# First batch of a pooled attention in quarters of half the heads by half the tokens, with keys pooled in turned form

## The chip, the cores and the metric

The kernel runs on one core of one Trainium2 chip. The metric is the device time in microseconds (us) of one execution; of several runs the median is given. Engine names as in the profile: PE is TensorE (matmuls) and PEld its weight loads, DVE is VectorE, ACT is ScalarE, POOL is GpSimd, SP is SyncE. PSUM is the memory that PE writes its results to, in eight banks of 512 fp32 columns; SBUF holds all else.

## What is computed

Eight batches of eight heads, 576 tokens and 64 columns a head go through an attention whose keys and values are first pooled: each row of the pooled keys is the mean of 8 tokens, so 72 rows are left. The result, as 4608 tokens by 512 columns, goes through four experts, each with two products, weighted by normed probabilities.

```python
k_p = k.reshape(B, H, Sp, pool, D).mean(axis=3)          # 72 rows of 8 tokens each
v_p = v.reshape(B, H, Sp, pool, D).mean(axis=3)
scores = scale * np.matmul(q, k_p.transpose(0, 1, 3, 2))
...
attn = np.exp(scores)
attn = attn / (np.sum(attn, axis=-1, keepdims=True) + 1e-09)
return np.matmul(attn, v_p).astype(np.float32)
...
p = domain_probs / (domain_probs.sum(-1, keepdims=True) + 1e-09)
for e in range(E):
    h = np.maximum(x @ w1[e], 0.0)
    out += p[:, e:e + 1] * (h @ w2[e])
```

## The kernel before

The tokens are worked on in nine chunks: the first 512 tokens of each of the eight batches, and a ninth chunk of the 64 left over from each. For a chunk, x is held turned (xT: columns on the partitions, in four blocks KC of 128), so that the up product of an expert gives the hidden values H with the hidden columns on the partitions, and the down product gives rows of the output, which DVE, ACT or POOL add to an accumulator with the probability as a factor. From the second chunk on, the products of an expert go by seven steps with sums of blocks (`up_product`, L680, and `down`, L749). The attention of the next batch is mixed into the products of the present one by slots. All engines work in the order in which the code issues to them; nothing is reordered.

The first batch has no products beside it to be mixed into. `attention_first` (L552) writes its order out by hand, for all engines, from the landing of the queries to the up product of the first expert. It is all that the change rewrites.

- *Loads.* Queries come as fp32 over the queues of SP and ACT (`load_q`, L174) and are rounded to bf16 by DVE and ACT (`round_q`, L188). Keys and values of the first batch (`load_first`, L135), then all weights, come over POOL's queue in the order of lines 1035 to 1048; most of POOL's issues after 15 us wait for an earlier one to land.
- *Queries.* `queries` (L343) turns them on PE, two heads a bank, and DVE and ACT copy them to `qT`.
- *Keys.* The 576 tokens of a head lie as 64 rows of 9 tokens, two heads of a group on partitions 0 to 63 and two on 64 to 127. `sum_pool` (L308) pools them with a matrix of zeros and ones (`takes`) as weights: 9 steps for each of the two halves, 18 matmuls a group of four heads (L314), which give pooled rows on 72 partitions. `sum_keys` (L320) casts them to `kp_all`, each key twice side by side; `keys` (L295) turns four heads with four PE transposes (L304) and one copy (L306) into `kpT`, which then has the key's 64 columns on partitions 0 to 63 and once more on 64 to 127. A query head has its tokens in the same two halves, so scores of both halves are made by matmuls on the two halves of the array's rows.
- *Scores.* `scores_first` (L531) makes the scores of four heads (a group) and half the tokens (256) in two banks, 8 matmuls, and one exp on ACT (L547). There are four such steps, taken in turn in the two-bank tiles `att` and `att_first`.
- *Contexts.* A context is 128 tokens by all heads (`context`, L456): 8 matmuls, then `divide` (L419) with a reciprocal and a multiply on DVE. For the first 128 tokens it goes by halves of the heads (`context_half`, L430). `turn` (L471) and `turn_half` (L444) turn the result on PE and copy it to xT, on ACT or DVE.
- *The first expert's up product.* `up_first` (L625) takes 128 tokens at a time for hidden blocks in pairs, and for the first 128 tokens also half the columns of x at a time, so that it can begin as soon as half the heads are there. In all 96 matmuls of 128 columns (L634) and, by `up`, 16 of 256 (L617).
- `idle` (L329) issues matmuls on zeros, 13 while the queries are loaded, and 1 and 3 more in between.

The eight banks are, before: `att` (two), `unit10` and `unit11`, the two `chains`, and `att_first` (two), which is given back after the first batch and becomes `unit00` and `unit01`.

Behind it stands `first_chunk` (L874) with the other experts' products of the first chunk. Its first matmul is that of the second expert (L617, into a bank of `units` or `chains`).

Of the kernel before, what the change touches and what calls it, by code (L numbers as in the profile page):

```python
# [17 lines left out]
def kernel(  # L18
# [10 lines left out]
    nc = tc.nc  # L29
# [36 lines left out]
    units = [None, [psum.tile([P, NT], F32, name=f"unit1{i}") for i in range(2)]]  # L66
    chains = [psum.tile([P, NT], F32, name=f"o_ps{i}") for i in range(2)]
    psum_first = tc.tile_pool(name="psum_first", bufs=1, space=bass.MemoryType.PSUM)
    att_first = [att, psum_first.__enter__().tile([P, 2, NT], F32, name="att_first")]
# [185 lines left out]
    def turn_of(what, n):  # L255
        turns[what] += 1
        return turns[what] % n
# [4 lines left out]
    def work_bank():  # L262
        return units[1][turn_of("work", 2)][:]

# [30 lines left out]
    def keys(b, hs):  # L295
# [6 lines left out]
        kpt_ps = (chains[1][:] if b else spare_bank()).bitcast(BF16)[:, 0:H * SP].rearrange("p (h j) -> p h j", j=SP)  # L302
        for h in range(hs.start, hs.stop):
            nc.tensor.transpose(kpt_ps[:, h, :], kp_all[0:SP, h], ident[:SP, :SP])  # L304
        copy = nc.scalar.copy if b else nc.vector.tensor_copy
        copy(out=state[("kpT", b)][:, hs, 0:SP], in_=kpt_ps[:, hs])  # L306
# [13 lines left out]
    def sum_keys(g, banks):  # L320
        copies = (nc.scalar.copy if g else nc.vector.tensor_copy, nc.scalar.copy)
        for copy, (hs, kp) in zip(copies, sum_pool("kraw", g, banks), strict=True):
            copy(out=kp_all[0:SP, hs], in_=kp.unsqueeze(2).to_broadcast([SP, 2, 2, D]))

    def sum_values(g, banks):
        for hs, vp in sum_pool("vraw", g, banks):
            nc.vector.tensor_copy(out=vps[0][:, hs, 0:D], in_=vp)

    def idle(n, w_ps=None, cols=NT):  # L329

        if w_ps is None:
            w_ps = work_bank()
        for _ in range(n):
            nc.tensor.matmul(w_ps[:, 0:cols], lhsT=zeros[:, 0:P], rhs=zeros[:, 0:cols])
# [41 lines left out]
    def key_columns(b, h, lo):  # L376

        return state[("kpT", b)][:].rearrange("p h j -> p (h j)")[lo:lo + D, h * SPT:h * SPT + P]
# [51 lines left out]
    def context_half(r, g, bank):  # L430

        if g == 0:
            state[("x", 0, r)] = npool.tile([P, 2, NPAIR, D], BF16, name="x_tok", bufs=4)
        c_ps = bank.rearrange("p (a n) -> p a n", a=1)
        for i in range(NPAIR):
            at = i * (D + 1)
            nc.tensor.matmul(
                c_ps[:, 0, at:at + D + 1],
                lhsT=state[("expT", 0)][:, g * NPAIR + i, r // 2, r % 2, :],
                rhs=vps[0][:, g * NPAIR + i, :], skip_group_check=True,  # L440
            )
        divide(c_ps, state[("x", 0, r)][:, g:g + 1])

    def turn_half(r, g, bank):  # L444
        if ("xT", 0) not in state:
            state[("xT", 0)] = xpool.tile([P, KC, NT], BF16, name="xT")
        x_tok = state[("x", 0, r)][:].rearrange("p a h d -> p (a h d)")
        ks = slice(g * HK, (g + 1) * HK)
        xt_ps = bank.bitcast(BF16)[:, 0:HK * P].rearrange("p (k t) -> p k t", t=P)
        for i in range(HK):  # L450
            kc = g * HK + i
            nc.tensor.transpose(xt_ps[:, i, :], x_tok[:, kc * P:(kc + 1) * P], ident[:])
        copy = nc.scalar.copy if g else nc.vector.tensor_copy
        copy(out=state[("xT", 0)][:, ks, r * P:(r + 1) * P], in_=xt_ps)
# [16 lines left out]
    def turn(b, r):  # L471
# [7 lines left out]
        xt_ps = (units[1][0][:] if b else att_first[1][:, 0] if r == 3 else chains[0][:]).bitcast(BF16)[:, 0:KC * P].rearrange("p (k t) -> p k t", t=P)  # L479
        for kc in range(KC):  # L480
            nc.tensor.transpose(xt_ps[:, kc, :], x_tok[:, kc * P:(kc + 1) * P], ident[:])
        copy = nc.vector.tensor_copy if b == 0 and r == 3 else nc.scalar.copy
        copy(out=dst, in_=xt_ps)
# [68 lines left out]
    def attention_first():  # L552

        lo, hi = groups(0)
# [570 lines left out]
```

## Time and profile before

| | |
|---|---|
| median of 3 runs | 489.5 us (489.46 to 489.64) |
| the profiled execution | 489.29 us |
| its span, from the first to the last instruction | 487.3 us |
| PE, DVE, ACT busy | 480.4, 378.4, 305.2 us |
| DMA, bytes moved in the span | 41.98 MB, 86 GB/s on average |
| the exps of the first batch (L547), start of the first and of the fourth | 10.60 and 13.64 us |
| PE on the products of the first expert (L634, L617), first start | 13.95 us |

Times inside the execution are counted from the start of the span. A row of the timeline gives start, length, engine, line, operation, output and input with their shapes, how many instructions it merges, and in brackets the idle time of the engine before it and what ended that. Matmuls are pipelined: a row's length includes the way of the last one through the array, so that a row of n matmuls is longer than n times their distance. The chain of waits is followed back from the last instruction: each step names what the next one waited for, or what stood ahead of it on the same engine. The 40 slices give the busy share of an engine in tenths.

### The profile page before, as it was taken

Reading aid. Unit: us, or ns where it says so; the run is one execution under the profiler, and the core shown is the slowest. Engines: PE = TensorE matmul, PEld = TensorE weight load, DVE = VectorE, ACT = ScalarE, POOL = GpSimd, SP = SyncE. Lnnn points to the kernel's source line nnn. Section 1 sums busy time; section 2 is a strip of 40 time slices with the busy share of each in tenths; the row PEclk is TensorE's granted clock in tenths of the full one; section 3 lists DMA queues with packets and bytes.
Section 4 is the critical chain, followed back from the end, with each engine's and each line's share of the span. In section 5 each row is a group of like instructions: output and inputs, shape, how many; then the busy total and the mean of one; then the engine's idle time right before and its main releaser. Section 6 shows DMA issues by size and latency. Waiting matters only on the chain.

```text
span 487.3 us, 11610 instructions
## 1 busy us (share of the span) xinstructions
PE 480.4 (99%) x4717; PEld 412.2 (85%) x4721; DVE 378.4 (78%) x763; ACT 305.2 (63%) x584; POOL 120.5 (25%) x121
## 2 busy tenths in 40 slices
PE   8999999999999999999999999999999999999996
PEld 4868578898888888888888889888888888888885
DVE  5689799999768976797679866997678766876674
ACT  4887446855676567656765667556755566556650
POOL 8440504242523154016411452111011101010000
PEclk9999999999999999999999999999999999999999
DMA  9999999976976689245945297311111010003003
GB/s 200 206 209 203 201 156 173 97 87 56 114 102 57 86 83 144 32 87 56 159 48 90 26 163 69 69 23 66 35 23 23 23 66 3 12 23 86 1 1 88
DMA packets 102981, 41.98 MB, mean 86 GB/s; under 512 B 73984, under 2 KB 102400, under 8 KB 102928
## 3 DMA queue, kind: packets, MB, share of 16 engines
q0 software_dynamic: 58064, 22.42, 41.4%
q1 hardware_dynamic: 43744, 17.77, 17.2%
q10 hardware_dynamic: 1120, 1.05, 0.6%
q8 instruction: 37, 0.61, 0.5%
q14 instruction: 16, 0.13, 0.1%
HBM read 45.69 MB, written 9.44 MB: 113 GB/s over the span
## 4 chain that ended last, share of the span: by engine, by line
PE 96%; ACT 1%; DMA 1%; DVE 1%; issue 0%
PE unit L698 42%; PE o_ps L766 41%; PE o_ps L792 3%; PE att L463 2%; PE unit L825 1%; DMA acc<-in_q_dram 1%; PE o_ps L617 1%; PE att L388 1%; PE unit L617 1%; PE unit L634 1%; PE unit L388 1%; ACT qT L374 0%; PE o_ps L634 0%; PE att L517 0%; PE att L500 0%; PE unit L314 0%
## 5 line engine op out<-in xcount | busy, mean ns | idle before, releaser
L845 DVE SCALAR_TENSOR_TENSOR acc<-o_ps,p_all,acc 128x256 f32<-128x256 f32 (+1 forms) x285 | 127.0, 486 | 52.6 <-PE o_ps L766 36.6
L766 PEld LDWEIGHTS <-H 128*128 128x128 bf16 x1320 | 129.1, 98 | 15.0
L698 PEld LDWEIGHTS <-w_bf 128*128 128x128 bf16 x1088 | 105.2, 98 | 13.0 <-issue 0.2
L678 DVE CUSTOM_DVE_ANT_0 H<-unit,partial 128x512 bf16<-128x512 f32 x128 | 87.3, 685 | 24.2 <-PE unit L698 13.3
L766 PE MATMUL o_ps<-w_bf,H 128*128 128x256 bf16 x792 | 102.6, 272 | 0.0
L698 PE MATMUL unit<-xT,w_bf 128*128 128x256 bf16 x704 | 100.5, 273 | 0.0
L780 POOL TENSOR_TENSOR acc<-acc,addend 128x512 f32<-128x512 f32 x24 | 30.4, 1266 | 250.4 <-ACT addend L778 211.4
L713 ACT COPY partial<-unit 128x512 f32<-128x512 f32 x128 | 72.2, 591 | 30.3 <-PE unit L698 30.2
L698 PEld LDWEIGHTS <-wu_bf 128*128 128x128 bf16 x816 | 77.6, 98 | 11.6 <-issue 2.5
L698 PE MATMUL unit<-xs,wu_bf 128*128 128x256 bf16 x512 | 77.0, 273 | 0.0
L766 PE MATMUL o_ps<-wt_bf,H 128*128 128x256 bf16 x528 | 68.4, 273 | 0.0
L715 ACT ACTIVATE H<-unit 128x512 bf16<-128x512 f32 x66 | 39.9, 606 | 31.2 <-PE unit L698 31.2
L766 PEld LDWEIGHTS <-S 128*128 128x128 bf16 x528 | 51.7, 98 | 6.0
L719 ACT ACTIVATE H<-unit 128x512 bf16<-128x512 f32 x66 | 39.6, 601 | 25.7 <-PE unit L698 25.4
L711 ACT COPY unit<-unit 128x512 f32<-128x512 f32 x68 | 39.4, 582 | 23.6 <-PE unit L698 18.0
L698 PE MATMUL unit<-xs,w_bf 128*128 128x256 bf16 x256 | 38.4, 273 | 0.0
L843 ACT ACTIVATE acc<-o_ps,p_all 128x256 f32<-128x256 f32 x72 | 30.6, 484 | 9.4 <-PE o_ps L766 7.9
L154 POOL DMA_DIRECT2D kraw<-in_k_dram x20 | 26.4, 1320 | 40.2 <-DMA kraw<-in_k_dram 40.2
L698 PE MATMUL unit<-xT,wu_bf 128*128 128x256 bf16 x240 | 35.7, 272 | 0.0
L766 PE MATMUL o_ps<-w_bf,S 128*128 128x256 bf16 x264 | 34.2, 273 | 0.0
L766 PE MATMUL o_ps<-wt_bf,S 128*128 128x256 bf16 x264 | 34.2, 273 | 0.0
L154 POOL DMA_DIRECT2D vraw<-in_v_dram x20 | 28.6, 1431 | 19.9 <-DMA vraw<-in_v_dram 14.6
(157 smaller groups left out, 510.3 us busy)
## 6 DMA issues: line engine op xcount, KB each, us to landing
out_dram<-acc SPq DMA_DIRECT2D x32, 256.0 KB, 4.7
w_bf<-in_moe_w_dram POOLq DMA_DIRECT2D x11, 512.0 KB, 12.9
q_sb<-in_q_dram POOLq DMA_DIRECT2D x7, 512.0 KB, 10.5
vraw<-in_v_dram POOLq DMA_DIRECT2D x22, 144.0 KB, 6.2
kraw<-in_k_dram POOLq DMA_DIRECT2D x21, 144.0 KB, 6.0
w_bf<-in_moe_w_dram POOLq DMA_DIRECT2D x2, 1024.0 KB, 14.0
wt_bf<-in_k_dram POOLq DMA_DIRECT2D x4, 144.0 KB, 5.6
wt_bf<-in_v_dram POOLq DMA_DIRECT2D x4, 144.0 KB, 4.2
```

The costliest lines, as they stand in the source:

```text
L154: nc.gpsimd.dma_start(out=raw[:], in_=rows_of(src, b, 2 * part, 2 * part + 2), accum_op=ALU.add if part else ALU.bypass)
L678: nc.vector._custom_dve(TENSOR_ADD_SAT, out=dst, in0=ps, in1=part, s0=LARGEST, s1=0.0)
L698: nc.tensor.matmul(ps[:, n * HN:(n + 1) * HN], lhsT=lhs[:, kc, f:f + P], rhs=rhs[:, kc, :], start=(not grows and n == 0 and kc == 0), stop ...
L711: nc.scalar.copy(out=banks[1][:], in_=ps)
L713: nc.scalar.copy(out=part[:, step - 2], in_=ps)
L715: nc.scalar.activation(out=quarter(0, 0), in_=ps, func=ACT.Relu)
L719: nc.scalar.activation(out=quarter(0, 1), in_=ps, func=ACT.Relu)
L766: nc.tensor.matmul(ps[:, j], lhsT=lhs[:, i, j * P:(j + 1) * P], rhs=rhs[:, i, :], start=(not grows and i == 0 and j == 0), stop=(i == HF - 1),
L780: nc.gpsimd.tensor_add(out=dst, in0=dst, in1=addend[:])
L792: nc.tensor.matmul(o_ps, lhsT=lhs, rhs=w2_bf[:, e, fc, :], start=(fc == 0), stop=(fc == FCH - 1), skip_group_check=True,)
L843: nc.scalar.activation(out=dst, in_=o_ps, func=ACT.Copy, scale=prob)
L845: nc.vector.scalar_tensor_tensor(out=dst, in0=o_ps, scalar=prob, in1=dst, op0=ALU.mult, op1=ALU.add,)
```

## The change

- `sum_keys` pools the keys in turned form: the raw keys of one head are the weights (64 rows by 64 columns) and the matrix `takes` is streamed (72 columns). A group takes 36 matmuls instead of 18, gives 64 partitions of pooled, turned keys in a two-bank tile, and two copies put them on partitions 0 to 63 and 64 to 127 of the key tiles. For the first group the copies are DVE's and ACT's and go to two different tiles (`kpTs[0]` and `kpTs[2]`); for the second both are DVE's and go to `kpTs[1]`. The casts to `kp_all` and the PE transposes are gone for the first batch.
- A new two-bank tile `work_first` in the pool of the first batch takes the place of `unit10` and `unit11` there. These two are made with `unit00` and `unit01` after the first batch.
- Contexts, turns and the up product of the first expert go by quarters: 256 tokens (t) by four heads (g). A quarter of the context has 8 matmuls and one `divide` over 128 partitions by 512 columns; its turn has four transposes and one copy, always on ACT; the product of a quarter has 8 matmuls of 256 columns into two banks, and four hidden blocks stay open in PSUM until the second half of the heads has come. The other four hidden blocks take all 512 tokens at once, 16 matmuls.
- The values' copies are DVE's for the first group and ACT's for the second.

```diff
     def sum_keys(g, banks, copies):
+        for r in range(ROWS):
+            for hh in range(2):
+                for half in range(2):
+                    ps = slice(half * PR, (half + 1) * PR)
+                    nc.tensor.matmul(
+                        banks[0:D, half, hh * SP:(hh + 1) * SP], lhsT=raws[("kraw", 0)][ps, g, hh, r, :],
+                        rhs=takes[ps, r], start=(r == hh == 0), stop=(r == ROWS - 1), skip_group_check=True,
+                    )
+        for dup, copy in enumerate(copies):
+            copy(out=keys_first(g, dup)[dup * D:(dup + 1) * D, 4 * g:4 * g + 4, 0:SP].rearrange(
+                     "p (b h) j -> p b h j", b=2),
+                 in_=banks[0:D, :, 0:2 * SP].rearrange("p b (h j) -> p b h j", j=SP))
...
+    def context_quarter(t, g, c_ps):
+        for r2 in range(2):
+            for i in range(NPAIR):
...
+        x_tok = state[("x", 0, t, g)] = npool.tile([P, 2, NPAIR, D], BF16, name="x_tok", bufs=4)
+        divide(c_ps, x_tok)
...
+    def turn_quarter(t, g, bank, copy):
...
+        xt_ps = bank.bitcast(BF16)[:, 0:HK * HN].rearrange("p (k r t) -> p k r t", r=2, t=P)
+        for r2 in range(2):
+            for i in range(HK):
+                nc.tensor.transpose(
+                    xt_ps[:, i, r2, :], x_tok[:, r2, 2 * i:2 * i + 2].rearrange("p h d -> p (h d)"), ident[:])
+        copy(out=state[("xT", 0)][:, g * HK:(g + 1) * HK, t * HN:(t + 1) * HN],
+             in_=xt_ps.rearrange("p k r t -> p k (r t)"))
...
+    def up_quarter(t, g, banks):
...
+        for fc in range(HF):
+            for kc in range(g * HK, (g + 1) * HK):
+                nc.tensor.matmul(
+                    banks[fc // 2][:, fc % 2 * HN:(fc % 2 + 1) * HN],
+                    lhsT=w1_bf[:, 0, kc, fc * P:(fc + 1) * P], rhs=xT[:, kc, at],
+                    start=(fc % 2 == kc == 0), stop=(kc == KC - 1), skip_group_check=True,
+                )
+        for pair in range(2 * g):
+            nc.scalar.activation(
...
     def attention_first():
...
-        sum_keys(0, work)
-        idle(3, A2[:, 0], P)
-        sum_keys(1, [B2[:, 0], B2[:, 1]])
-        keys(0, lo)
-        scores_first(0, 0, A2)
-        keys(0, hi)
-        sum_values(0, work)
-        scores_first(1, 0, B2)
-        context_half(0, 0, chains[1][:])
-        scores_first(0, 1, A2)
-        sum_values(1, work)
-        turn_half(0, 0, chains[1][:])
-        scores_first(1, 1, B2)
-        context_half(0, 1, chains[0][:])
-        context(0, 1, A2)
-        up_first(range(0, 2), first, range(0, HK))
-        turn_half(0, 1, chains[0][:])
-        context(0, 2, B2)
-        up_first(range(2, 4), first, range(0, HK))
-        turn(0, 1)
-        up_first(range(0, 4), first, range(HK, KC))
-        context(0, 3, A2)
-        turn(0, 2)
-        up_first(range(0, 4), second)
-        turn(0, 3)
-        up_first(range(0, 4), third)
-        up_first(range(0, 4), fourth)
-        up_first(range(4, FCH), first)
-        up_first(range(4, FCH), second)
-        up(0, 0, range(4, FCH), half)
+        sum_keys(0, W2, (vector, scalar))
+        idle(3, B2[:, 1], P)
+        scores_first(0, 0, A2)
+        sum_keys(1, W2, (vector, vector))
+        scores_first(0, 1, B2)
+        scores_first(1, 0, A2)
+        sum_values(0, [W2[:, 0], W2[:, 1]], vector, vector)
+        scores_first(1, 1, B2)
+        context_quarter(0, 0, W2)
+        context_quarter(1, 0, A2)
+        sum_values(1, [C0, C1], scalar, scalar)
+        turn_quarter(0, 0, W2[:, 0], scalar)
+        context_quarter(0, 1, B2)
+        turn_quarter(1, 0, W2[:, 1], scalar)
+        up_quarter(0, 0, (C0, C1))
+        context_quarter(1, 1, A2)
+        turn_quarter(0, 1, B2[:, 0], scalar)
+        up_quarter(1, 0, (W2[:, 0], W2[:, 1]))
+        turn_quarter(1, 1, A2[:, 0], scalar)
+        up_quarter(0, 1, (C0, C1))
+        up_quarter(1, 1, (W2[:, 0], W2[:, 1]))
+        for fc, bank in enumerate((B2[:, 0], A2[:, 0], C0, C1), HF):
+            up(0, 0, (fc,), bank=bank)
```

In this order `B2` is the tile `att`, `A2` is `att_first`, `W2` is `work_first`, `C0` and `C1` are the two `chains`.

## The prediction

> **What bounds the kernel now.** I read the busy totals and the 40 slices first, then the chain of waits, then the timeline of the first 24 us, then the waits on DMA.
>
> ```profile
> PE 480.4 (99%) x4717; PEld 412.2 (85%) x4721; DVE 378.4 (78%) x763; ACT 305.2 (63%) x584; POOL 120.5 (25%) x121
> ...
> PE   8999999999999999999999999999999999999996
> ```
>
> TensorE (PE) is busy from the second slice to the last, so a microsecond that it loses in the first slices comes out at the end. All that changes lies before 23.32 us. There the chain, which has a start, a length and an owner in each row, passes from engine to engine:
>
> ```profile
> 6.55 0.54 DVE q_sb L194
> ...
> 9.80 0.32 DVE kpT L306
> ...
> 10.17 0.40 PE att_first L543 x8
> ...
> 11.47 0.29 DVE vp L327
> ...
> 16.53 0.35 PE o_ps L481 x4
> 16.88 0.89 PE unit L634 x16
> ...
> 23.32 0.21 PE o_ps L617
> ```
>
> Up to about 16 us it is made of hand-overs (the queries rounded, keys turned, values copied); from 16.53 it is PE alone. The row at 23.32 is the first matmul of the second expert. No code behind it is changed, except for which bank stands where, so I compare the two kernels at that point. What may not come any earlier is shown by the timeline further on:
>
> ```profile
> 34.30 0.69 DVE L250 TENSOR_TENSOR wt_bf<-w_bf,wt_bf 128x1024 bf16<-128x1024 bf16 x1 [0.63 <-DMA w_bf<-in_moe_w_dram]
> ...
> 34.43 1.03 PE L766 MATMUL o_ps<-w_bf,H 128*128 128x256 bf16 x8
> ```
>
> VectorE (DVE) waits until 34.30 for the second half of the first expert's down weights, and PE reads the same half at 34.43. The DMA queues move about 205 GB/s from 6 us to there and their order isn't changed. So PE has 0.13 us in hand: **a gain ahead of this point is worth at most 0.13 us, while a loss counts in full.**
>
> **The keys.** Before, a group of four heads takes 18 matmuls (L314), a cast that doubles each key, four transposes and a copy. After, it takes 36 matmuls that give the turned keys at once, and two copies (partitions 0 to 63 and 64 to 127).
>
> ```profile
> 7.68 0.70 PE L314 MATMUL unit<-wt_bf,S 64*72 64x128 bf16 x18
> ...
> 8.41 0.42 DVE L323 CAST kp<-unit 72x256 bf16<-72x256 f32 x1
> ...
> 9.46 0.30 PE L304 MATMUL o_ps<-ident,kp 72*128 72x72 bf16 x4
> ...
> 9.80 0.31 DVE L306 COPY kpT<-o_ps 128x288 bf16<-128x288 bf16 x1 [0.97 <-PE o_ps L304]
> ...
> 10.60 1.02 ACT L547 ACTIVATE expT<-att_first 72x1024 bf16<-72x1024 f32 x1 [0.40 <-PE att_first L543]
> ```
>
> The new matmuls (64 rows by 64 columns of weights, 72 columns streamed) have no row. From 0.70 us for 18 less one matmul's 0.216 come 28 ns for each L314, half of the 56 ns that 128 columns take alone (L634, 16 in 0.89): the two row halves of the array run side by side. In slices of 4 ns, the two of a pair start 4 ns apart, pairs 56 ns. 72 columns alone take (0.30 - 0.20) / 3 = 33 ns (L304). So 18 pairs at 33 ns are 0.59 us a group. Bounds: side by side with nothing but streaming, 0.54; one after the other, 36 x 33 ns = 1.19. I take 0.59: the nearest row, L314, has the same two row halves.
>
> [...]
>
> A copy of 288 columns: DVE rows of 0.285 us for 128 and 0.421 for 256 fp32 columns give 0.455; ScalarE (ACT) at 0.385 for 256 and 0.597 for 512 gives 0.41. In the built order ACT's copy of the first group waits for DVE's, since both read one PSUM tile, so they add up. I follow the path with 0.03 to 0.06 us a hand-over, as between the rows above.
>
> - First group: sums from 7.68, end 8.44; DVE 8.47 to 8.93; ACT 8.96 to 9.37; scores 9.42 to 9.81 (as the 0.40 row); first exp 9.84, against 10.60.
> - Second group's sums 9.65 to 10.44. Scores of the first group's second half follow on PE, end 10.77; exp 10.82. DVE's two copies, 10.47 to 11.32; scores 11.37 to 11.80; third exp 11.84. Fourth: an exp follows another after 0.92, so 12.76 to 13.78.
>
> Before, the fourth ended at 13.64 + 1.02 = 14.66. **Keys and scores gain 0.88 us.** The second group's sum lies on this path as well.
>
> **The quarters.** Before, PE has something to do between the exps and just after (half contexts, half products of the first expert). After, a context is two blocks for half the heads, and its chain is: 8 matmuls (0.42), reciprocal 0.20, multiply 0.69, 4 transposes (0.40), and a copy that is always ACT's (0.59). From the rows:
>
> - values of group 0 copied by DVE, to 12.82; context (0,0) 12.87 to 13.29, divided by 14.24; context (1,0) divided behind it on DVE, by 15.15.
> - values of group 1 summed by PE to 14.17 (behind both contexts), copied by ACT to 14.60. Queued behind these copies on ACT: the turn of (0,0), 14.78 to 15.37.
> - the turn of (1,0) waits for that copy, as it writes another bank of the same tile: PE 15.42, ACT to 16.44. That is the last wait which PE feels much.
> - from 15.65 PE has, nearly without a gap: four quarter products of 8 x 110 ns (3.5), context (1,1) (0.26), two turns (0.23 each), 16 matmuls of 512 columns at 216 ns (3.45), some 0.06 for gaps: 7.7 us. End 23.38.
>
> So **from the last exp to the second expert it takes 9.60 us, against 23.32 - 14.66 = 8.66: 0.94 lost.** The products themselves are 0.17 us less (before 96 x 56 ns + 16 x 109 = 7.12; after 32 x 109 + 16 x 216 = 6.95), and it is in this sum.
>
> At nothing: DVE's sums of the turned batch and of the first expert's up weights (from 18.57) start 0.4 us later and are hidden by its 2.21 us of idle time ahead of 24.38 (a wait on the probabilities' DMA); without that cover, all of DVE's later sums would come 0.4 us later, which PE meets at its first products with sums, from 31.8. ReLU copies (0.60 each per 0.86 us of PE) fit. SP and POOL issue nothing different, and no load waits on what moves.
>
> **Sum.** -0.88 + 0.94 = +0.06. The same adding-up on the order of before reaches the second expert 0.43 us too early; 0.24 of it arises up to the fourth exp, mostly in the second key sum (0.84 where 0.70 is usual), which the new order starts 1 us later; the remaining 0.2 I add. So +0.26: 489.29 (the profiled execution, 487.3 of span and 2.0 around it) becomes 489.55. The median of the runs stands 0.21 above that execution: **489.8 us**.
>
> **Rivals.**
>
> 1. *The row halves don't overlap* in the 64-column form. Place: both key sums. Price 2 x (1.19 - 0.59) = 1.2 us, all on the path to the exps, so +1.46: 491.0, slower. It decides from about 27 ns a matmul, where the loss passes 1 us. For: no row has this shape. Against: L314 and L543 both run in pairs. 15%.
> 2. *Hand-overs cheaper than I add them* (no 0.2, copies overlapped): the chain would reach the second expert up to 0.3 us early, and the weights give back all but 0.13: 489.4. For: the 0.2 is a remainder that I can't place. 14%.
> 3. *The clock falls.* By the steps above PE idles more in the new stage (some 0.5 us in each of six places between 8.5 and 15.4). The 13 warm-up matmuls of 512 columns start 0.43 us apart until 4.2 us and 0.216 later in the kernel, so a half-speed state exists, though the granted-clock slices read 9 throughout. If 3 us of the quarters ran at that speed: +1.5, so 491.3. Against: the stage before has idle gaps too, and its rows stay at 56 ns. 4%.
>
> [...]
>
> The forecast itself has 64% (489.4 to 490.2, with tails); 3% is left for a gain over 0.2%, which would need weights that land earlier. A difference of 0.2% (1.0 us) is about what a measurement of this kernel can tell from no change. Slower by more: rivals 1 and 3, and 2% of the forecast's tail, 21%. Faster by more: 3%. Within: 76%. The range reaches from rival 2 into the lower part of rival 1: 489.3 to 490.8.
>
> **What would show it.** In the changed profile: 36 key matmuls in about 0.8 us (1.4 if rival 1 is right); the first exp near 9.84 and the fourth's end near 13.8; the turn copies on ACT near 15, 16, 17.5 and 18.5; the first matmul of the second expert near 23.4 to 23.6; PE without idle time from there, and the down product at 34.43 not earlier than 34.3. I am wrong if the second expert starts after 24.3, or if the first half of the weights no longer sets the limit at 34.3.

## The result

| | before | after |
|---|---|---|
| median | 489.57 us (489.42 to 489.99, 6 runs) | 492.31 us (491.96 to 492.61, 6 runs) |
| span of the profiled execution | 487.3 us | 490.3 us |
| start of the key sums | 7.68 us | 8.05 us |
| end of the fourth exp | 14.66 us | 14.35 us |
| first matmul of the second expert | 23.16 us | 23.96 us |
| first matmul of L825, near the end | 476.21 us | 479.05 us |

The changed kernel is slower: the ratio is 1.0055, 95% interval 1.0042 to 1.0068. The forecast was 489.8 us with a range from 489.3 to 490.8, so it missed. (The start of the second expert is taken here from the rows of the timeline, 23.16 before and 23.96 after; the prediction's 23.32 is the same matmul in the chain, which begins the step when the matmul ahead has ended, and there it is 24.13 after.)

```profile
23.16 1.03 PE L617 MATMUL o_ps<-xT,w_bf 128*128 128x512 bf16 x3
```

```profile
23.96 1.03 PE L620 MATMUL unit<-xT,w_bf 128*128 128x512 bf16 x4
```

Busy totals and slices of the changed kernel's page:

```profile
PE 481.0 (98%) x4680; PEld 410.4 (84%) x4685; DVE 377.4 (77%) x757; ACT 304.6 (62%) x577; POOL 120.5 (25%) x121
...
PE   8999998999999999999999999999999999999996
```

PE has 37 matmuls less and is still the bound. The slice that fell from 9 to 8 is the seventh, from 74 to 86 us: far behind the code that was rewritten. The list of PE's waits behind 20 us is empty for the kernel before. For the changed one it has two entries (who waits, for whom, us in total, times, longest):

```profile
PE att L510 <- DMA kpT<-kp: 1.5, 1, 1.5
PE unit L698 <- ACT unit L711: 0.2, 1, 0.2
```

**The first entry** is the scores of the 64 remaining tokens of batches 0 and 1. PE's timeline, and the chain of waits around it (start, length, owner):

```profile
80.82 0.20 PE L510 MATMUL att<-qTr,kpT 64*128 64x64 bf16 x1
82.53 0.40 PE L510 MATMUL att<-qTr,kpT 64*128 64x64 bf16 x15 [1.51 <-DMA kpT<-kp]
```

```profile
78.21 4.27 DMA kpT<-kp
...
82.53 0.40 PE att L510 x15
```

The same step of the kernel before, on its timeline:

```profile
79.67 0.41 PE L500 MATMUL att<-qTr,kpT 64*128 64x64 bf16 x16
```

There the 16 matmuls run at once. In the changed kernel the first one runs and the second waits for the transfer that brings batch 2's keys; PE loses 1.70 us by it. The reason is in lines of the change that the cut of its diff further up does not show, so that "It is all that the change rewrites", said there of the opening, does not hold:

```diff
+    def keys_first(g, dup):
+
+        return kpTs[1] if g else kpTs[2 * dup]
...
     def key_columns(b, h, lo):
 
-        return state[("kpT", b)][:].rearrange("p h j -> p (h j)")[lo:lo + D, h * SPT:h * SPT + P]
+        kpT = state[("kpT", b)] if b else keys_first(h // NPAIR, lo // D)
+        return kpT[:].rearrange("p h j -> p (h j)")[lo:lo + D, h * SPT:h * SPT + P]
```

The first group's second copy of batch 0's keys goes to `kpTs[2]`, and the second group's keys to `kpTs[1]`; `key_columns` is also what the scores of the remaining tokens read. Batch b's keys go to `kpTs[b % 3]`, so `kpTs[2]` is written by batch 2 while batch 0's remaining tokens still have to be scored. Before, all of batch 0's keys were in `kpTs[0]`, which is not written again until batch 3. What the changed kernel computes is changed by it too: of batch 0's remaining tokens, heads 1 and 3 are scored with batch 2's keys, and heads 4 to 7 with batch 1's. PE waits there for keys that it should not read at all.

**The second entry** is a short stop at 42 us. The chain of the changed kernel there:

```profile
40.24 1.30 DVE partial L678 x2
41.54 0.02 issue
41.56 0.02 ACTq L711
41.58 0.38 issue
41.95 0.58 ACT unit L711
```

The copy at L711 starts 0.38 us after all that it waits for; before, it started 0.09 us after the same work of DVE (which ended at 40.72). PE's next work (the same L698 at 41.43 before and 42.58 after) is 0.35 us later by it.

The 3.0 us of the spans come apart by rows, each later start against the one ahead of it: 0.37 ahead of the key sums, 0.43 from there to the second expert, 0.35 at 42 us, 1.70 at 81 us. Together 2.85; the first matmul of L825, nearly 400 us further, is 2.84 later. In between nothing is added or given back. The 0.37 belongs to this execution: the same code starts the key sums at 7.52 to 7.55 us in the profiles of three other kernels with quarters, told below.

### The profile page after: what moved, and what is told of

It is laid out like the page before. It is cut to its first block, busy times and chain, and to the rows that moved or that the text cites. A ratio compares the mean times of both kernels' runs of the same rounds, so it can differ in the third digit from the quotient of the medians.

```text
span 490.3 us, 11521 instructions
## 1 busy us (share of the span) xinstructions
PE 481.0 (98%) x4680; PEld 410.4 (84%) x4685; DVE 377.4 (77%) x757; ACT 304.6 (62%) x577; POOL 120.5 (25%) x121
## 4 chain that ended last, share of the span: by engine, by line
PE 95%; DVE 2%; ACT 1%; DMA 1%; issue 0%; DVEq 0%; ACTq 0%
PE unit L698 41%; PE o_ps L766 40%; PE o_ps L792 3%; PE att L474 2%; PE unit L825 1%; PE work_first L345 1%; PE o_ps L620 1%; PE att L400 1%; DMA kpT<-kp 1%; PE unit L620 1%; PE unit L400 1%; ACT qT L385 0%; DVE acc L845 0%; PE work_first L634 0%; PE o_ps L634 0%
## 5 line engine op out<-in xcount | busy, mean ns | idle before, releaser
L698 PEld LDWEIGHTS <-w_bf 128*128 128x128 bf16 x1088 | 105.2, 98 | 13.3 <-issue 0.6
L698 PE MATMUL unit<-xT,w_bf 128*128 128x256 bf16 x704 | 100.5, 272 | 0.2 <-ACT unit L711 0.2
L698 PEld LDWEIGHTS <-wu_bf 128*128 128x128 bf16 x816 | 77.6, 98 | 11.7 <-issue 2.5
L698 PE MATMUL unit<-xs,wu_bf 128*128 128x256 bf16 x512 | 77.0, 273 | 0.0
L711 ACT COPY unit<-unit 128x512 f32<-128x512 f32 x68 | 39.4, 582 | 23.9 <-PE unit L698 18.0
L698 PE MATMUL unit<-xs,w_bf 128*128 128x256 bf16 x256 | 38.4, 273 | 0.0
L843 ACT ACTIVATE acc<-o_ps,p_all 128x256 f32<-128x256 f32 x72 | 30.6, 484 | 9.2 <-PE o_ps L766 7.5
L698 PE MATMUL unit<-xT,wu_bf 128*128 128x256 bf16 x240 | 35.7, 272 | 0.0
L156 POOL DMA_DIRECT2D vraw<-in_v_dram x20 | 27.9, 1397 | 18.4 <-DMA vraw<-in_v_dram 17.5
```

The costliest lines, as they stand in the source:

```text
L156: nc.gpsimd.dma_start(out=raw[:], in_=rows_of(src, b, 2 * part, 2 * part + 2), accum_op=ALU.add if part else ALU.bypass)
L698: nc.tensor.matmul(ps[:, n * HN:(n + 1) * HN], lhsT=lhs[:, kc, f:f + P], rhs=rhs[:, kc, :], start=(not grows and n == 0 and kc == 0), stop ...
L711: nc.scalar.copy(out=banks[1][:], in_=ps)
L843: nc.scalar.activation(out=dst, in_=o_ps, func=ACT.Copy, scale=prob)
```

## Experiments

Each compares medians with runs of the kernel before on the same chip (489.48 to 489.63 us). The 12 are told in groups. Those made from the changed kernel with `kpTs[1]` still in use, and the two wait-alone kernels, score part of batch 0's remaining tokens with another batch's keys; the others compute what is meant.

### Does the key tile cost the wait?

**The first group's second copy goes home.** In the changed kernel:

```diff
     def keys_first(g, dup):
-        return kpTs[1] if g else kpTs[2 * dup]
+        return kpTs[1] if g else kpTs[0]
```

> The changed kernel with one edit: both copies of the first group's keys go to the tile kpTs[0]; the second copy no longer goes to kpTs[2], which batch 2's keys are written to later. The scores of the 64 remaining tokens of batch 0 (L510) then read no tile that batch 2's transfer writes. As in the changed kernel they still take batch 1's keys for heads 4 to 7, so that part of the output is not the reference's. Theory A (the tile that the second copy stands in makes PE wait 1.51 us for a transfer at 80.8 us): the wait goes, and nothing else of it was covered, so the time falls by 1.5 to 1.9 us, from 492.3 to 490.4 to 490.8; in the profile PE has no idle time over 0.2 us between 70 and 100 us. Rival B (PE is late there for another reason, or the stall only moves to the next thing that is late): at most 0.4 us less, 491.9 to 492.3, and another idle time of about 1.5 us behind 80 us. Rival C (the loss of the opening is what counts and is merely seen there): no change, 492.3.

Measured: 490.26 us (490.09 to 490.88, 11 runs), ratio to before 1.0013 (1.0005 to 1.0022). Against the changed kernel that is 2.05 us less. All its waits of PE behind 20 us:

```profile
PE unit L698 <- ACT unit L711: 0.2, 1, 0.2
```

The wait on the transfer is gone and nothing took its place: theory A. The second group's keys, still in `kpTs[1]`, cost nothing, since batch 1's keys are written by a copy at 49.9 us and nobody waits for them at 80.

**The wait alone, in the kernel before.**

```diff
-        return state[("kpT", b)][:].rearrange("p h j -> p (h j)")[lo:lo + D, h * SPT:h * SPT + P]
+        kpT = kpTs[2] if late and h < NPAIR and lo else state[("kpT", b)]
+        return kpT[:].rearrange("p h j -> p (h j)")[lo:lo + D, h * SPT:h * SPT + P]
...
-                        lhsT=key_columns(2 * i + bb, 2 * pair + hh, lo),
+                        lhsT=key_columns(2 * i + bb, 2 * pair + hh, lo, late=(i == bb == 0)),
```

> The kernel before with one edit: the scores of batch 0's remaining tokens read the keys of heads 0 to 3 for the second partition half from kpTs[2] (batch 2's keys, so that part of the output is not the reference's) instead of kpTs[0]; the opening is untouched. Theory A: this adds the wait for batch 2's keys alone; PE reaches these scores at 79.7 us and the transfer landed at 82.5 us in the changed kernel and started right behind work that stands at the same place, so 1.5 to 2.7 us are lost, 491.1 to 492.3. Rival B (the wait costs only because the changed opening shifts PE against the DMA queues): under 0.4 us, 489.6 to 490.0.

Measured: 489.72 us (489.34 to 490.69, 11 runs), ratio 1.0005 (0.9996 to 1.0013). Theory A missed by over 1 us; the time lies where rival B had put it. On PE's timeline the 16 scores take 0.63 us in place of 0.41, so the wait is there, but it is 0.2 us:

```profile
79.77 0.63 PE L501 MATMUL att<-qTr,kpT 64*128 64x64 bf16 x16
```

The transfer was issued at 77.16 and landed 2.8 us later; in the changed kernel it took 4.27. The dependency alone does not make 1.7 us; the other half is that the transfer is slow in the changed kernel.

### Why is the transfer slow there?

In the profiles of the two kernels and of the first ten experiments (some are told further down) a queue of the program's own instructions (q8, `instruction` in the profile) moves 16 KB about every 13 us. In the DMA view of the changed kernel, cut to the time of the transfer (queue, packets, MB, share; then issues with their median time to landing):

```profile
q8 instruction: 1, 0.02, 1.5%
q14 instruction: 1, 0.01, 0.7%
...
kpT<-kp SPq DMA_TRANSPOSE x1, 4.3
```

The same view of the kernel before, cut to its transfer:

```profile
q1 hardware_dynamic: 1176, 0.66, 81.7%
q0 software_dynamic: 397, 0.10, 40.2%
...
kpT<-kp SPq DMA_TRANSPOSE x1, 3.3
```

In the changed kernel a 16 KB load of instructions (q8) starts at 80.14, inside the transfer; in the kernel before there is none. It starts there at 74.46, inside the transposition of the remaining queries, issued at 73.27. In all these twelve profiles the one of these two transfers that had such a load in it took 3.8 to 4.5 us, and the other one 2.45 to 3.3. The order of before has the load on the queries, for which PE does not wait; the quarters have it on the keys. This can be tested without touching any of the code around 80 us: by the number of matmuls.

**The load moved off the transfer, in the changed kernel.**

```diff
-        idle(13, W2[:, 0])
+        idle(55, W2[:, 0], 96)
```

> The changed kernel with 55 warm-up matmuls of 96 columns in place of 13 of 512; nothing else. In all twelve profiles so far the queue of the program's own instructions moves 16 KB at a time, about every 13 us; of the two small transposes near 75 and 80 us, the one in which such a load falls takes 3.8 to 4.5 us from issue to landing and the other 2.45 to 3.3. In the order before the load falls at 73 to 76 us (the remaining queries), in quarters, which have 37 matmuls less, at 78.6 to 81 us (batch 2's keys, the ones that PE waits for). Theory A (PE's instruction load, moved by the count of matmuls, makes the transfer slow, and so the wait long): 42 matmuls more bring the load to 75.5 to 77 us; the transfer takes 2.6 to 3.3 us, PE waits 0 to 0.6 us at L510 in place of 1.5, and the time falls by 1.0 to 1.6 us, 490.7 to 491.3. Rival B (the transfer is slow for a reason that lies in the quarters' order): 4 us and more, a wait of 1.5 us, 492.1 to 492.6.

**The load moved onto the transfer, in the wait-alone kernel.**

```diff
-        idle(13)
+        idle(98, cols=64)
```

> The converse: the wait-alone kernel (489.72 us; part of batch 0's remaining tokens scored with batch 2's keys, as there) with 98 warm-up matmuls of 64 columns in place of 13 of 512. Theory A: 85 matmuls more bring the next instruction load, at 88.2 us in that profile, to 78 to 80 us, into the transfer of batch 2's keys; it takes 3.9 to 4.5 us in place of 2.8, PE waits 1.2 to 1.8 us for it in place of 0.2, and the time rises by 1.0 to 1.6 us, 490.7 to 491.3. Rival B: the transfer takes 2.7 to 3.3 us and the time stays, 489.5 to 490.0.

Measured: the changed kernel with the load moved 490.39 us (490.05 to 490.74, 11 runs), ratio 1.0016 (1.0007 to 1.0025): 1.92 us less than the changed kernel, from the warm-up matmuls alone (in the profiles 0.48 us of it is an earlier start of the key sums, 7.57 in place of 8.05, and the rest the wait). The wait-alone kernel with the load moved 491.98 us (491.21 to 494.09, 6 runs), ratio 1.0060 (1.0042 to 1.0079). In three of its six executions the mean granted clock was 0.992 to 0.995; the other three are 491.21 to 491.40, that is 1.5 to 1.7 above the wait alone. The DMA views, cut to the transfer: of the first,

```profile
q1 hardware_dynamic: 766, 0.26, 46.0%
q0 software_dynamic: 85, 0.02, 10.1%
...
kpT<-kp SPq DMA_TRANSPOSE x1, 2.7
```

and of the second, with its only wait of PE behind it:

```profile
q8 instruction: 1, 0.02, 1.3%
...
kpT<-kp SPq DMA_TRANSPOSE x1, 4.3
```

```profile
PE att L501 <- DMA kpT<-kp: 1.5, 1, 1.5
```

In the first the load starts at 75.39 and the transfer takes 2.7 us; PE has no wait there. In the second it starts at 79.65, inside, and the transfer takes 4.3. This is theory A both times by the profiles; the times moved by more than its 1.0 to 1.6 us (1.92 down, and 2.26 up, or 1.5 to 1.7 in the executions at full clock). Four kernels and the two originals make a square:

| | load elsewhere | load in the transfer |
|---|---|---|
| PE does not read the tile | before, 489.5 | first group home, 490.26 (the transfer took 4.2 us, nobody waited) |
| PE reads the tile | wait alone, 489.72; changed with load moved, 490.39 | **changed, 492.31**; wait alone with load moved, 491.98 |

Both are needed.

*How* a load of 16 KB, itself 1.0 us long, makes the transfer 1.5 us longer is shown in part by the single packets of the traces. The transfer consists of 640 packets of 256 bytes. In the changed kernel 629 of them have started by 80.39 and the last 11 only from 81.14 on; the load's one packet lasts from 80.14 to 81.15. In the wait-alone kernel with the load moved, 639 have started by 79.63 and the last at 80.52; the load's packet ends at 80.53. Two more of the seven kernels with a load in this transfer show the same, and none of the seven without. So the last packets seem to stand behind the load's; that they share an engine with it is not recorded. From the last such packet to the landing it is 1.03 us in the changed kernel and 0.48 in its version with the load moved; why stays open.

A load is not the only thing that makes a transposing transfer long either: the next one, `x_rem` (issued between 91 and 96 us), takes from 2.42 to 6.36 us in the 14 profiles, and no 16 KB load starts in it in any.

The kernel before has 37 of these 16 KB loads, and no wait of PE behind 20 us with them. The cost is seen where PE waits for a transfer that meets one: 4.3 us from issue to landing in the changed kernel, 2.7 in its version with the load moved.

### What is the 0.38 us at 42 us?

In the trace the copy at L711 that starts late is ACT's 64th instruction (the sequencer's counted). It is late by 0.37 to 0.38 us in all five kernels that have quarters and no ACT instruction more or less. In the kernel before, whose ACT has seven instructions more by then, the 64th is an activation of L843 with 0.86 us of idle time ahead of it; it starts (37.25) 0.02 us behind the PE work that it waits for.

**Three instructions more on ACT**, in the first-group-home kernel:

```diff
         idle(13, W2[:, 0])
+        for n in range(3):
+            nc.scalar.copy(out=act_pad[:, n:n + 1], in_=zeros[:, 0:1])
```

> The first-group-home kernel (490.26 us) with three copies of one column on ACT ahead of the queries' rounding, where ACT has 2.9 us of idle time. In the three profiles with quarters, ACT's 64th instruction starts 0.377 us after everything that it waits for; it is the copy at L711 that PE waits for at 42 us, and PE stands still for 0.2 us and shifts by 0.33. In the kernel before, the 64th is one of the 0.47 us activations at L843, behind an idle time of 0.86 us. Theory A (the delay belongs to the 64th instruction of the engine, whichever it is): with three more the 64th is an L843 with idle time ahead of it, PE has no wait at 42 us, and the time falls by 0.3 us, 489.8 to 490.1. Rival B (the delay belongs to the copy itself, for instance to its PSUM bank, since the units' banks are made in another order): PE still waits 0.2 us for L711 and the time stays at 490.2 to 490.4.

Measured: 490.07 us (489.74 to 490.54, 11 runs), ratio 1.0012 (1.0003 to 1.0020). PE has no wait left behind 20 us, and the copy, now ACT's 67th instruction, follows DVE's work (39.98 to 41.27) by 0.09 us, as it did before:

```profile
41.36 1.06 ACT L714 COPY unit<-unit 128x512 f32<-128x512 f32 x2 [0.98 <-DVE partial L681]
```

So the delay does not belong to the copy itself, and rival B is out. That it belongs to the 64th instruction is theory A's reading and is not shown by itself: the 64th is here an activation at L846 that starts right behind the one ahead of it, with no delay to be seen. In the time it is 0.19 us, where 0.3 was expected; with spreads of 0.8 us the two kernels are not told apart by it. The next delay of this kind in the kernel before, on ACT at 340.5 us, is the 576th instruction, 512 further. No run says more about why.

### What do the keys and the quarters cost by themselves?

**Quarters with all keys at home**, the changed kernel with `kpTs[0]` for both groups, whose second copies then stand behind the first group's second scores:

```diff
-        return kpTs[1] if g else kpTs[2 * dup]
+        return kpTs[0]
...
         scores_first(0, 1, B2)
+        copy_keys(1, W2, (vector, vector))
```

> The changed kernel with all keys of batch 0 in kpTs[0]; the second group's copies stand behind the first group's second scores, since both groups now share a tile. It computes what the reference does. Theory A (quarters cost 0.25 to 0.45 us in the opening, and the tile that the keys stand in costs the 1.7): 490.2 to 490.9, no wait of L510 on a transfer, second expert at 23.5 to 24.2. Rival B (something in the quarters beside the tile costs over 1 us): 491.5 or more. Rival C (the quarters are no loss): 489.3 to 489.8.

Measured: 491.21 us (490.66 to 492.58, 5 runs), ratio 1.0033 (1.0020 to 1.0045). Between A and B. There is no wait on the transfer, but a new loss. Windows of 1 us on PE (start and end; length, PE busy and matmuls, granted clock, DMA share, GB/s):

```profile
11.00:12.00 1.00, 0.33 (x5) 1.00 1.18 184
...
14.00:15.00 1.00, 1.00 (x21) 0.57 1.22 199
15.00:16.00 1.00, 1.00 (x14) 0.50 1.26 210
...
17.00:18.00 1.00, 1.00 (x10) 0.72 1.24 207
```

PE is idle for two thirds of a microsecond at 11, and from 14 us the granted clock is at a half for 3 us. This is the prediction's third rival, in a kernel next to the changed one. The changed kernel itself does not show it: its clock reads 1.00 in every such window, with 0.45 busy at 11. Here it came in some executions only: the five have mean granted clocks of 1.000, 1.000, 0.999, 0.996 and 0.993, and the last two are the two longest, 491.48 and 492.58 us.

**The idle time filled**, in that kernel:

```diff
         scores_first(0, 1, B2)
+        idle(8, C0, P)
...
         scores_first(1, 1, B2)
+        idle(5, C0, P)
         context_quarter(0, 0, W2)
```

> The quarters-home kernel (491.21 us, 490.66 to 492.58) with 8 and 5 matmuls on zeros (128 columns, 56 ns each) in the two places where PE waited 0.6 and 0.35 us between 10.8 and 13.4 us. In its profile the granted clock was 0.57, 0.50, 0.50 and 0.72 in the microseconds from 14 to 18; PE was busy 0.33 of the microsecond from 11. Theory A (PE's idle time there lets the clock fall, in some executions): the clock stays at 1.00 from 14 us, the spread shrinks to that of the kernel before (about 1 us), and the median falls by 0.3 to 0.6 us, 490.6 to 490.9. Rival B (the fall has nothing to do with these idle times): median and spread stay, 491.0 to 491.4, with executions up to 492.5.

Measured: 490.69 us; seven of eight runs from 490.51 to 491.06, one 492.75; ratio 1.0029 (1.0018 to 1.0040). The median is 0.52 lower, the profile shows 1.00 in every such window, and no execution has a mean granted clock below 0.998: this fits theory A, but for the one run, which the clock does not explain. It is not shown: the intervals of the two kernels overlap, and three of the five executions without the filling had a mean of 0.999 or 1.000 too.

**Turned keys alone, twice.** In the kernel before, keys are pooled in turned form, all into `kpTs[0]`, and contexts, turns and products stay. In the first trial the fourth scores stood behind `turn_half`:

```diff
+        sum_keys(0, work)
+        copy_keys(0, work)
         idle(3, A2[:, 0], P)
         scores_first(0, 0, A2)
+        sum_keys(1, work)
+        scores_first(0, 1, B2)
+        copy_keys(1, work)
+        scores_first(1, 0, A2)
         sum_values(0, work)
...
         turn_half(0, 0, chains[1][:])
         scores_first(1, 1, B2)
```

> The kernel before with the keys alone in turned form: 36 matmuls a group, two copies a bank (DVE one bank, ACT the other), all keys of batch 0 in kpTs[0]; contexts, turns and the first expert's product as before. It computes what the reference does. Theory A (the turned sums shorten the path to the exps; a gain there is cut off at the weights that land at 34.3 us): the fourth exp ends 0.6 to 0.9 us earlier counted from the start of the key sums, the second expert starts 0.5 to 0.9 us earlier, PE then has an idle time of 0.3 to 0.8 us ahead of the down products of 34 us, and the total is 0.1 to 0.4 us less: 489.2 to 489.5. Rival B (the weights are no limit, since the down products can be as early as the rest): the whole 0.7 comes out, 488.7 to 488.9. Rival C (the gain is used up by the tail of hand-overs before the second expert): second expert at 23.2 to 23.4, total 489.5 to 489.8.

Measured: 492.64 us (490.52 to 493.98, 8 runs), ratio 1.0047 (1.0028 to 1.0066). No theory foresaw it, and it says nothing on the keys: the fourth exp started at 16.12 only, since its scores waited behind a turn that waits for a division, and the clock stood at 0.50 from 14 to 20 us. The executions part by the clock: the five with a mean of 0.990 to 0.993 took 492.38 to 493.98 us, the three with 0.998 to 1.000 took 490.52 to 490.80. So the second trial:

```diff
         scores_first(0, 1, B2)
+        copy_keys(1, work, (nc.vector.tensor_copy, nc.vector.tensor_copy))
+        sum_values(0, [bank[:] for bank in chains])
         scores_first(1, 0, A2)
+        scores_first(1, 1, B2)
         context_half(0, 0, chains[1][:])
```

> The kernel before with keys alone in turned form, as in the first trial (492.64 us), but ordered so that PE is not idle: the sums of the first group's values stand between the first group's scores and the second group's, all four copies of the second group's keys are DVE's, and the fourth scores follow the third at once. It computes what the reference does. Theory A (the turned keys gain at the exps, and what comes out at the end is what the weights that land at 34.3 us leave): fourth exp ends 0.3 to 0.6 us earlier than in the kernel before, counted from the start of the key sums, second expert 22.8 to 23.2, clock at 1.00, time 489.1 to 489.5. Rival B (the order of the values costs it again): second expert 23.3 to 23.8, 489.5 to 490.1. Rival C (the clock falls here too): 491 or more, with a spread of 2 us.

Measured: 489.35 us (489.04 to 490.81, 11 runs), ratio 1.0001 (0.9993 to 1.0010): the same as before. The time lies where A put it, but A's mechanism is not there. The fourth exp ends at 13.98, 6.59 us behind the start of the key sums (7.39) where 6.98 was usual; the second expert starts at 23.20, which is 15.81 behind it where 15.48 was usual. DVE's and PE's timelines say what is late next:

```profile
10.56 1.06 DVE L335 CAST kpT<-unit 64x144 bf16<-64x144 f32 x4 [1.52 <-PE att L556]
11.65 0.49 DVE L340 CAST vp<-o_ps 72x128 bf16<-72x128 f32 x2
```

```profile
12.19 0.29 PE L450 MATMUL o_ps<-vp,expT 72*128 72x65 bf16 x4
```

The values' copies stand behind four copies of keys, and the first context starts 4.80 us behind the key sums, against 4.12 before (11.80 to 7.68). What the exps gain is, by these rows, lost at the values; no run moves the values' copies alone.

**The quarters at their best**: all keys at home, the first values' sums in PE's idle time, and the three copies of one column:

```diff
         copy_keys(1, W2, (vector, vector))
+        sum_values(0, [C0, C1], vector, vector)
         scores_first(1, 0, A2)
```

> The quarters-home kernel with the sums of the first group's values on PE between the scores of the two groups, where PE was idle 0.6 us (in place of matmuls on zeros), and three copies of one column on ACT as padding. It computes what the reference does. Theory A (the wait on the transfer, the idle time that lets the clock fall, and the 64th instruction are what the change lost; the quarters themselves are within 0.3 us of the old order): 489.4 to 490.0, second expert at 23.2 to 23.6, no wait of PE over 0.1 us behind it. Rival B (the quarters' tail of copies and divisions costs 1 us more than the old order): 490.3 or more.

Measured: 490.31 us (489.80 to 490.57, 11 runs), ratio 1.0013 (1.0004 to 1.0022). Just over the line to B, though not for B's reason: the second expert starts 15.78 us behind the key sums, 0.30 over the usual. In this execution PE then waited 0.54 us at 70 us, behind a DVE sum that had waited 0.9 us for weights at 65.6. That is a limit by the weights as the prediction had in mind, at another place.

### The start of the key sums

The 0.37 us ahead of the key sums comes from code that the change does not touch. In ten profiles the 13 warm-up matmuls took 4.27 to 5.73 us from the same start, 5.73 in the changed kernel's. In the kernel before they start 0.43 us apart up to 4.22 us and 0.216 from 4.51 on, in the changed kernel 0.43 apart to the last. That a clock rises in between, as the expectation below has it, is an inference from these distances; the granted clock reads 1.00 in every window from 1 to 6 us of both.

**Eleven in place of thirteen**, in the kernel before and in the second turned-keys kernel:

```diff
-        idle(13)
+        idle(11)
```

> The kernel before with 11 warm-up matmuls in place of 13. In ten profiles so far the 13 took 4.27 to 5.73 us from 1.26, since they start 0.43 us apart until the clock rises and 0.216 behind that; where they took over 5.2 us, they ended after the first queries were rounded, and the turns of the queries started at 6.44 to 6.78 in place of 6.00 to 6.16. The executions of the kernel before lie in two groups, 489.0 to 489.5 and 489.7 to 490.3. Theory A (the slower group is that of the late clock, in which the warm-up matmuls keep PE from the queries): 11 of them end by 6.2 us in the worst case, the slower group goes, and the median falls by 0.1 to 0.3 us, 489.1 to 489.4, with nearly all executions under 489.6. Rival B (the groups have another cause): median and spread stay, 489.4 to 489.6. Rival C (two matmuls less leave PE idle longer ahead of the queries and the clock falls or rises later): 489.8 or more.

> The second turned-keys kernel (489.35 us, 489.04 to 490.81) with 11 warm-up matmuls in place of 13. It computes what the reference does. Theory A as for the kernel before: the slower executions go, median 489.0 to 489.3. Rival B: 489.3 to 489.6, unchanged. Rival C: 489.8 or more. If the turned keys are worth nothing at the end, it equals the kernel before with 11 within 0.2 us; if they are worth the 0.4 us by which the fourth exp is earlier, it is 0.3 to 0.4 us below that kernel.

Measured: 489.69 us (489.14 to 490.41) and 489.41 us (489.15 to 490.26), 11 runs each, ratios 1.0001 (0.9992 to 1.0009) and 0.9998 (0.9989 to 1.0007). This is nearest to rival B both times (the first lies 0.09 above its bounds): the spread of about 1 us stays, so its cause is not the warm-up matmuls, or not they alone, and stays open. The two kernels are not told apart: their medians differ by 0.28 us, and both intervals hold no difference from the kernel before. Whether the turned keys are worth a few tenths at the end is not shown. None of the twelve beats the kernel before.

## Why the prediction was wrong

**The step that failed** is in its first part: "All that changes lies before 23.32 us" and "No code behind it is changed, except for which bank stands where, so I compare the two kernels at that point". The order of the work behind the second expert is unchanged, but the change alters where data lie that this work reads. `key_columns` is in the diff, it is called by the scores of the remaining tokens, and the tiles it now names are rewritten by later batches. The later "no load waits on what moves" asks in one direction only: here PE waits for a load into what moved. In place of no cost behind 23.32 us there was 1.70 us in the trace and 2.05 us in the medians, the larger part of what was missed. No rival had it. Of the signs that were named, the second expert started before 24.3, as forecast; "PE without idle time from there" is the one that failed.

**That the wait would be so long** was not in the rows of before: there the transfer is issued at 77.06 and lands at 80.36, 0.7 us behind the scores at 79.67. By these rows the wait would have been estimated at 0.7 us, and the experiment with the wait alone gave 0.2. The rest came with the load of instructions inside the transfer, and the number of matmuls moves that load: it starts at 80.14 us in the changed kernel, which has 37 matmuls less than the kernel before, and at 75.39 with 42 more.

**The 0.35 us at 42 us** was not foreseen either; no step of the prediction counted instructions. Its cause stays open.

The steps on the opening stand by themselves, measured from the start of the key sums:

- *Key sums.* Forecast about 0.8 us, measured in the timeline of the changed kernel:

```profile
8.05 0.77 PE L324 MATMUL work_first<-S,wt_bf 64*64 64x72 bf16 x36
...
9.37 0.23 PE L553 MATMUL att_first<-qT,kpT 64*128 64x128 bf16 x1 [0.28 <-DVE kpT L329]
...
11.51 0.23 PE L553 MATMUL att_first<-qT,kpT 64*128 64x128 bf16 x1 [0.29 <-DVE kpT L329]
11.99 0.39 PE L553 MATMUL att_first<-qT,kpT 64*128 64x128 bf16 x7 [0.26 <-DVE kpT L329]
```

  (0.77 - 0.20) / 36 is 16 ns a matmul. The two of a pair start 2 to 4 ns apart and the pairs 32 to 34 (53 from the first to the second), so the row halves run side by side, and rival 1 is out. (The 4 ns between the two of a pair, which the prediction gives for L314, hold for the values' sums; in the row that it quotes they are 8 to 10.) The prediction's bound of 0.54 us for a group can be worked out from the starts of matmuls of 128 and of 512 columns, 56 and 216 ns apart: 0.417 ns a column, an estimated 30 ns for 72.
- *First exp.* Forecast 2.16 us behind the start of the sums, measured 2.17 (10.22).
- *Fourth exp.* Forecast to end 6.10 behind it, measured 6.30, before 6.98: a gain of 0.68 in place of 0.88. The third scores wait for DVE's two copies one after the other (11.51 and 11.99), which began 2.95 behind the start and not 2.79, and took 0.93 us and not 0.85.
- *Turn copies.* Forecast near 15, 16, 17.5 and 18.5, measured 15.34, 16.40, 17.76 and 18.96, with a start that was 0.37 later. The last exp and the first and last of the copies on ACT's timeline:

```profile
13.34 1.01 ACT L557 ACTIVATE expT<-att 72x1024 bf16<-72x1024 f32 x1
...
15.34 0.59 ACT L464 COPY xT<-work_first 128x512 bf16<-128x512 bf16 x1
...
18.96 0.58 ACT L464 COPY xT<-att_first 128x512 bf16<-128x512 bf16 x1 [0.62 <-PE att_first L462]
```

- *From the last exp to the second expert.* Forecast 0.94 and the remainder of 0.2, so 1.14 more than before; measured 9.61 (14.35 to 23.96) against 8.50, so 1.11. The whole opening costs 0.43 where 0.26 was said.
- *The weights at 34.3 us.* In the changed kernel's profile DVE takes up the second half at 33.71 without waiting for it; in the others in which DVE waits for it, it lands between 33.3 and 34.3. A bound that was read from one execution to 0.13 us moved by 1 us in others. That a gain would be cut off there was never reached, since no version gained. That these weights (the second half; the prediction's last line says the first) no longer set the limit was named as a sign of being wrong. It came true in this profile, and has no part in the loss.
- *Rival 3, the clock.* It was given 4% and did not occur in the changed kernel, but in two related ones, the quarters with all keys at home and the first trial of turned keys. In the latter it went with 1.6 to 3.5 us more, near the price of 1.5 or above it. That PE's idle time brings it on is not shown: at 11 us PE was busy for 0.45 in that trial, as in the changed kernel, whose clock stayed. Nor is it shown that the warm-up matmuls, on which the rival leans, ran at half the clock: the granted clock reads 1.00 there.

## What to carry to other kernels

When a change puts data into another buffer, list every later reader and every later writer of that buffer to the end of the kernel before saying that nothing behind the edit is changed; a buffer that rotates has writers that no diff shows. A transfer that lands a few tenths ahead of or behind its reader is a wait whose size can depend on what else moves at that time: here it was 0.2 us with a transfer of 2.8 us and 1.5 with one of 4.3. The program's own instructions were part of it, and adding matmuls shifted them: 42 more took a load of 16 KB out of the transfer (from 80.14 to 75.39 us), 85 more in the wait-alone kernel brought one into it (79.65). And a gain at one mark (the exps) is a gain at the end only if what is late next (here, by the rows, the values' copies) has been moved too.

## What the runs showed of the hardware that was not expected

- A 16 KB load of the program's instructions inside a small transposing transfer went with about 1.5 us more for two of them: the remaining queries 2.44 to 2.46 us without and 3.8 to 4.0 with, batch 2's keys 2.7 to 3.3 without and 4.0 to 4.5 with, in 14 profiles of 14. Moving the load by the number of warm-up matmuls moved the length along: batch 2's keys from 4.3 to 2.7 us in the changed kernel, and from 2.8 to 4.3 in the wait-alone kernel.
- Single instructions started late with nothing to wait for that the profile shows: ACT's 64th by 0.37 to 0.38 us in five kernels; the 576th on ACT or DVE in some by 0.28 to 0.32 us (on ACT at 340.50 us in the kernel before, on DVE at 286.47 in the changed one). Three more ACT instructions ahead took the delay from the copy that had it (0.09 us in place of 0.38). That the place in the program decides fits these rows; it is not shown.
- Matmuls of 64 rows by 64 columns of weights and 72 streamed columns, alternating between the two row halves, took 16 ns each ((0.77 - 0.20) / 36, L324 of the changed kernel).
